# mLSTM with top-1 MoE: list scatters once per group, and transposed columns through a PSUM bank of their own

## The chip, the core and the metric

The kernel runs on one core of a Trainium2 chip. The core has a matmul engine (TensorE, PE in the profile; PEld is its weight load), three engines for element-wise work (VectorE or DVE, ScalarE or ACT, GpSimd or POOL) and SyncE (SP), which here only starts transfers. Each engine runs its own instructions in order and waits on semaphores of the others. Matmuls write to PSUM, a small memory of banks, from which DVE and ACT read. POOL also issues the indirect transfers (gathers and scatters by a list of addresses).

The metric is the device time of one execution in microseconds (us). Lower is better.

## The reference

Two steps. First a recurrent attention (mLSTM) over 4 batches of 8 heads, 768 steps, 40 values per head. Then its output, as 3072 tokens of 320 values, goes through a mixture of experts that gives each token one of 8 experts, with a hidden width of 1024:

```python
logits = x @ w_gate + modality_bias[modality_id]
e_idx = np.argmax(logits, axis=1)
...
gate_w = probs[np.arange(N), e_idx]
for e in range(E):
    mask = e_idx == e
    h = np.maximum(x[mask] @ w1[e], 0.0)
    out[mask] = gate_w[mask, None] * (h @ w2[e])
```

`modality_id` is 0 or 1 for each token, and the bias of its modality mostly decides the expert.

## The kernel before

**Tiles.** Attention runs in 24 units of 128 rows and writes rows of x to DRAM (`x_d`), sorted by modality. As the bias mostly decides, the kernel does not wait for the logits: for each of the two modalities it deals six tiles of 256 tokens to that modality's usual expert, loads that expert's weights early, and multiplies while the logits are still being verified. The 12 dealt tiles are numbered 0 to 11 here. A token that turns out to want another expert (a "bad" one), and every token beyond the sixth tile of its modality, is entered in a list in DRAM (`list_d`), and two leftover tiles of 128 tokens ("slots") gather their tokens from it at the end, with weights that are loaded once the list says which experts they need.

**An expert tile** is 64 matmuls `h_ps` (L1012) in four chunks of 16, each followed by ACT's relu `hh` (L1015) and DVE's low part `hl` (L1016), then 48 matmuls `o_ps` (L1030) in four pieces of 12, and for each of its two halves of 128 tokens ACT's scaling `ob` (L841) and a scatter to `out` on POOL (L842). Between these eight pieces the code advances all other work once; such a step is a half-beat here, so a tile lasts eight of them.

**The work beside it** is a set of generators which `together()` advances once per half-beat each, in the order of the list `threads`. The order of the instructions on each engine is this order of writing: nothing moves them later. The ones that matter here:

- `load_work` loads a tile's tokens from `x_d` into `xg` (SP).
- `column_work(0)` and `column_work(1)`, for the even and odd tiles, run `column_steps`: ACT scales each half to a high part (`xr`/`ex`, L868), DVE makes the low part (two operations per half, L873), PE transposes five blocks into PSUM (`xTg_ps`, L480), and DVE copies them out as `xT` (L886). The transposes take a buffer of the pool `psY`, tag "y", of two buffers, which is also that of `o_ps`; `opend` and `y_last` keep a transpose from taking the second buffer while an `o_ps` is being summed.
- `verify_work` computes the logits of a group of tiles and marks `bad`; `list_work` runs `lists`, which ranks the bad tokens of the group by expert (matmuls L968 and L970, DVE L974 to L980) and scatters into `list_d`, one indirect transfer on POOL per half (L985). Addresses of tokens that aren't bad lie out of bounds and are dropped. The groups hold columns j = 0, 1, 2, 3, then 4 and 5 together, then 6 (the tokens beyond): 4 halves each, 8 in the fifth.
- `rest_work` waits for the last rank, computes the slots' expert numbers and counts (`work_list`, some 30 small DVE operations and the matmul of `nvds`, L721), then gathers the slots' tokens (L830) and makes their columns. `weight_work` starts the slots' weights as soon as the expert numbers are there: SP's transfers into `ws`, ACT's high part (L789), DVE's low part (L790).

If the list overflows what two slots can hold, a register `todo_i` sends the program into further code at its end. With the inputs used here it doesn't: four tokens in all are entered in the list, at most one of them in any partition of a group.

Of the kernel before, what the change touches and what calls it, by code (L numbers as in the profile page):

```python
# [20 lines left out]
P = 128  # L21
# [43 lines left out]
def kernel(  # L65
# [514 lines left out]
    def constants():  # L580
# [19 lines left out]
        g.memset(bases[:, NMOD:], float(NTOK))  # L600
        one_e = one_t[:, 0:E]
# [35 lines left out]
    def work_list(l, run, used, nk, nm):  # L637
# [80 lines left out]
        l.update(nv=nvi)  # L718
        yield "pe"
        nv_b = nvb[:, 0:nk]  # L720
        nc.tensor.matmul(nv_b, lhsT=ones[0:nk], rhs=nvd[0:nk, 0:nk], start=True, stop=True, skip_group_check=True)  # L721
# [5 lines left out]
        if nm == "s":  # L727


            nv_r, m = nv_b[0:1], cst.tile([1, 4], F32, name="more")  # L730
            v.tensor_copy(m[:, 0:1], nv_r[:, 2 * TS:2 * TS + 1])
            v.tensor_scalar(m[:, 1:2], nv_r[:, 0:1], -float(P), 0.0, ALU.add, ALU.max)
            v.tensor_tensor(m[:, 2:4], bases[0:1, 1:], ends[0:1], ALU.subtract)
            more = cst.tile([1, 1], F32, name="more1")
            v.tensor_reduce(more, m, axis=AX.X, op=ALU.max)
            v.tensor_scalar(todo_i, more, 1.0, None, ALU.min)
# [66 lines left out]
    def group(t, ks, js, nm):  # L803
# [4 lines left out]
                 ent=xp.tile([P, a, r, 2], I32, name="entr" + nm, bufs=1), mb=mb_sb[:, ks[0]:ks[0] + a], a=a, r=r, nm=f"{a}{r}", tls=[])  # L808
# [37 lines left out]
    def column_steps(tl, tight=False):  # L846


        nonlocal y_last
# [15 lines left out]
        if not tight:  # L865
            yield
        for h in range(nh):
            nc.scalar.mul(xrs[h][:, 0:DM], xg[:, h, 0:DM], sc[:, h:h + 1].bitcast(F32))  # L868
        if not tight:
            yield  # L870
        for h in range(nh):
            for a, z, o in ((2 * P, DM, DM), (0, 2 * P, 3 * P)):
                nc.vector.scalar_tensor_tensor(xrs[h][:, o:o + z - a], xg[:, h, a:z], sc[:, h:h + 1].bitcast(F32), xrs[h][:, a:z],  # L873
                                               ALU.mult, ALU.subtract)
        tl["split"] = True
        yield
        for h in range(nh):

            while opend and not y_last:
                yield  # L880
            ps = psY.tile([P, 5, P], F16, name="xTg_ps", tag="y")
            y_last = False
            transposes(xrs[h], ps)
            if not tight:
                yield
            nc.vector.tensor_copy(xT[:, :, h], ps)  # L886
        yield
# [63 lines left out]
    def lists(g, each=1):  # L951
# [27 lines left out]
        slot_i = sm.tile([P, n], I32, name="sloti" + nm)  # L979
        v.tensor_tensor(slot_i, slot, flat(off), ALU.add)  # L980
        g["ranked"] = True
        yield
        ent = g["ent"].rearrange("p a r w -> p (a r) w")
        for h in range(n):
            disjoint("list", nc.gpsimd.indirect_dma_start(  # L985
                out=list_d[:, :], out_offset=bass.IndirectOffsetOnAxis(ap=slot_i[:, h:h + 1].bitcast(U32), axis=0),
                in_=ent[:, h], in_offset=None, bounds_check=E * LCAP - 1, oob_is_err=False))
            if h % each == each - 1:
                yield

    h_pools = (psS, "s"), (psG, "g")

    opend = y_last = False
# [25 lines left out]
    def layer2(wts, tl, hid, halves):  # L1019

        nonlocal opend, y_last
        w2h, w2l = wts[2:4]
        hh, hl = hid
        for q, h in enumerate(halves):
            hs = slice(q * P, (q + 1) * P)
            o_ps = psY.tile([P, DM], F32, name="o_ps", tag="y")
            opend = y_last = True
# [9 lines left out]
            opend = False  # L1037
# [34 lines left out]
    run = cst.tile([P, E], F32, name="run")  # L1072

# [291 lines left out]
    def leftover():  # L1365

        v = nc.vector
        n = NTOK // T
# [53 lines left out]
    def still_state():  # L1422
# [183 lines left out]
        def load_work():  # L1606
            for x, (i, j, k) in enumerate(order):
# [5 lines left out]
                if i not in gs:  # L1613
                    gs[i] = group(tab, range(NMOD), sets[i], str(i))
# [7 lines left out]
        def column_work(q):  # L1622
            for x, (i, j, k) in enumerate(order):
# [8 lines left out]
                for _ in column_steps(tl, not over):  # L1632
# [15 lines left out]
        def list_work():  # L1648
            for i, js in enumerate(sets):
                while i not in gs or "verified" not in gs[i]:  # L1650
                    yield
                for _ in lists(gs[i], 2 if att_over else 1):
# [212 lines left out]
```

## Time and profile before

| | us |
|---|---|
| three runs | 326.4, 323.12, 323.44 |
| their median | 323.44 |
| the profiled execution | 320.36 |
| its span, first to last instruction | 318.6 |
| PE, DVE, ACT, POOL busy | 268.0, 169.9, 125.4, 121.0 |
| tile 6 starts | 176.10 |
| tile 10 starts | 260.10 |
| the slots' matmuls start | 290.8 |

A row of a timeline gives the start in us, the duration in us, the engine, the line, the operation with what it writes and reads, how many were merged, and in brackets the idle time ahead of it with what ended it. "<-issue" means that nothing in the profile explains the idle time, "<-remote" that the releaser couldn't be named. The granted clock of PE is 1 at full speed.

### The profile page before, as it was taken

Reading aid. Unit: us, or ns where it says so; the run is one execution under the profiler, and the core shown is the slowest. Engines: PE = TensorE matmul, PEld = TensorE weight load, DVE = VectorE, ACT = ScalarE, POOL = GpSimd, SP = SyncE. Lnnn points to the kernel's source line nnn. Section 1 sums busy time; section 2 is a strip of 40 time slices with the busy share of each in tenths; the row PEclk is TensorE's granted clock in tenths of the full one; section 3 lists DMA queues with packets and bytes.
Section 4 is the critical chain, followed back from the end, with each engine's and each line's share of the span. In section 5 each row is a group of like instructions: output and inputs, shape, how many; then the busy total and the mean of one; then the engine's idle time right before and its main releaser. Section 6 shows DMA issues by size and latency. Waiting matters only on the chain.

```text
span 318.6 us, 6393 instructions
## 1 busy us (share of the span) xinstructions
PE 268.0 (84%) x2384; PEld 210.8 (66%) x2384; DVE 169.9 (53%) x551; ACT 125.4 (39%) x230; POOL 121.0 (38%) x177
## 2 busy tenths in 40 slices
PE   8797986897999999897989959399997889979920
PEld 3475764885887889686866736387976468858810
DVE  7756786489473577329344546137531637775200
ACT  7427565375543455344132413022320226862200
POOL 8734452334755266442582103401137342303110
PEclk9999799799999999999999979789999599999995
DMA  6699968623561461051141411100001068851000
GB/s 176 169 287 335 279 199 272 229 70 114 167 186 62 127 187 41 23 158 53 41 127 41 128 40 36 50 0 23 23 2 41 0 176 197 278 204 43 2 11 0
DMA packets 17354, 36.63 MB, mean 115 GB/s; under 512 B 4439, under 2 KB 8505, under 8 KB 17314
## 3 DMA queue, kind: packets, MB, share of 16 engines
q1 hardware_dynamic: 13922, 27.90, 29.4%
q0 software_dynamic: 3392, 8.24, 7.6%
q8 instruction: 20, 0.33, 0.5%
q14 instruction: 20, 0.16, 0.2%
HBM read 27.90 MB, written 8.57 MB: 114 GB/s over the span
## 4 chain that ended last, share of the span: by engine, by line
PE 40%; DVE 17%; DMA 16%; issue 9%; ACT 6%; another core or an unknown queue 4%; POOL 3%; SPq 1%; POOLq 0%; ACTq 0%; DVEq 0%
PE o_ps L1030 15%; PE h_ps L1012 15%; DMA ws<-in_w 4%; DVE hl L1016 3%; DMA wx<-bp_d 3%; PE xTg_ps L480 3%; DMA kt<-in_kv 2%; PE y_ps L1488 2%; DMA sg<-in_og 2%; ACT hh L1015 2%; DVE ex L873 2%; DMA wx<-in_steps_c 2%; DVE wx L790 2%; PE ubank L892 1%
## 5 line engine op out<-in xcount | busy, mean ns | idle before, releaser
L1012 PEld LDWEIGHTS <-wx 128*128 128x128 f16 x896 | 82.8, 100 | 17.4 <-issue 7.4
L1030 PE MATMUL o_ps<-wx,hh 128*128 128x320 f16 x416 | 87.5, 304 | 3.3 <-DVE eb L886 1.9
L1016 DVE SCALAR_TENSOR_TENSOR hl<-h_ps,hh 128x512 f16<-128x512 f32 x52 | 35.8, 689 | 83.1 <-ACT hh L1015 58.1
L1012 PE MATMUL h_ps<-xT,wx 128*128 128x256 f16 x512 | 62.3, 280 | 2.9 <-DVE hl L1016 2.1
L1030 PE MATMUL o_ps<-wx,hl 128*128 128x320 f16 x208 | 63.0, 303 | 0.0
L1015 ACT ACTIVATE hh<-h_ps 128x512 f16<-128x512 f32 x52 | 30.9, 594 | 69.2 <-PE h_ps L1012 55.1
L842 POOL DMA_INDIRECT out<-ob,oi x24 | 25.7, 1069 | 83.5 <-ACT ob L841 75.7
L1030 PEld LDWEIGHTS <-hh 128*128 128x128 f16 x416 | 40.0, 100 | 19.4 <-issue 3.7
L1477 POOL TENSOR_TENSOR so<-sg,den 128x320 f32<-128x320 f32 x24 | 22.0, 915 | 58.2 <-DVE den L1473 45.9
L985 POOL DMA_INDIRECT list_d<-entr,sloti x28 | 27.9, 995 | 21.4 <-DVE key L927 9.8
L841 ACT ACTIVATE ob<-o_ps,entr 128x320 f32<-128x320 f32 x24 | 12.6, 526 | 56.3 <-PE o_ps L1030 53.9
L790 DVE SCALAR_TENSOR_TENSOR wx<-ws,wx 128x768 f16<-128x768 f32 (+1 forms) x24 | 26.8, 1125 | 8.7 <-ACT wx L789 5.8
L1140 PE MATMUL warm_ps<-warm 128*128 128x512 bf16 x101 | 27.4, 412 | 1.4 <-POOL neg L1197 1.4
L470 POOL DMA_INDIRECT x_d<-row,place_i x24 | 24.6, 1027 | 5.9 <-issue 4.3
L1030 PEld LDWEIGHTS <-hl 128*128 128x128 f16 x208 | 20.6, 99 | 8.4
L789 ACT ACTIVATE wx<-ws 128x768 f16<-128x768 f32 (+1 forms) x24 | 23.4, 978 | 6.0 <-DMA ws<-in_w 5.8
L1012 PE MATMUL h_ps<-eb,wx 128*128 128x256 f16 x192 | 23.4, 277 | 2.6 <-issue 2.6
L480 PE MATMUL xTg_ps<-ident_h,ex 128*128 128x128 f16 x110 | 11.0, 236 | 16.3 <-DVE eb L886 7.2
L480 PEld LDWEIGHTS <-ex 128*128 128x128 f16 x110 | 8.4, 106 | 19.2 <-issue 8.5
L1488 PE MATMUL y_ps<-wx,eb 80*128 80x82 f32 x160 | 20.8, 273 | 0.0
L1488 PEld LDWEIGHTS y_ps<-wx,eb 80*128 80x128 f32 x160 | 20.2, 194 | 0.8
L438 ACT ACTIVATE sg<-sg 128x960 f32<-128x960 f32 x16 | 15.9, 993 | 6.0 <-DMA sg<-in_og 5.9
(242 smaller groups left out, 305.5 us busy)
## 6 DMA issues: line engine op xcount, KB each, us to landing
ws<-in_w SPq DMA_DIRECT2D x16, 384.0 KB
ws<-in_w SPq DMA_DIRECT2D x8, 640.0 KB
xg<-x_d SPq DMA_DIRECT2D x14, 322.0 KB
sg<-in_og SPq DMA_DIRECT2D x8, 480.0 KB
eb<-in_ql SPq DMA_DIRECT2D x8, 320.0 KB
kt<-in_kv SPq DMA_DIRECT2D x4, 324.0 KB
wx<-in_qk SPq DMA_DIRECT2D x8, 160.0 KB
wx<-in_steps_c SPq DMA_DIRECT2D x2, 320.0 KB
```

The source lines that it names most:

```text
L470: ins = nc.gpsimd.indirect_dma_start(out=x_d[:, :], out_offset=bass.IndirectOffsetOnAxis(ap=place_i[:, n:n + 1].bitcast(U32), axis=0), in_ ...
L480: nc.tensor.transpose(dst[:, i], row[:, i * P:(i + 1) * P], ident_h)
L789: nc.scalar.mul(wh, w, WSC)
L790: lows.append(lambda wl=wl, w=w, wh=wh: nc.vector.scalar_tensor_tensor(wl, w, WSC, wh, ALU.mult, ALU.subtract))
L842: disjoint("out", nc.gpsimd.indirect_dma_start(out=out[:, :], out_offset=bass.IndirectOffsetOnAxis(ap=oi.bitcast(U32), axis=0), in_=ob, in ...
L985: disjoint("list", nc.gpsimd.indirect_dma_start(out=list_d[:, :], out_offset=bass.IndirectOffsetOnAxis(ap=slot_i[:, h:h + 1].bitcast(U32), ...
L1012: nc.tensor.matmul(h_ps[:, i], lhsT=l, rhs=r, start=(i == 0 and q == 0), stop=(i == g - 1 and q == 7), skip_group_check=True)
L1015: nc.scalar.activation(hh[:, sl, 0:n], h_ps, AF.Relu)
L1016: nc.vector.scalar_tensor_tensor(hl[:, sl, 0:n], h_ps, 0.0, hh[:, sl, 0:n], ALU.max, ALU.subtract)
L1030: nc.tensor.matmul(o_ps, lhsT=l[:, fc, hs], rhs=r[:, fc], start=(fc == 0 and i == 0), stop=(fc == NFC - 1 and i == 2))
L1140: nc.tensor.matmul(ps, lhsT=warm[:, 0:P], rhs=warm, start=True, stop=True, skip_group_check=True)
L1488: nc.tensor.matmul(y_ps[:, 2 * p:2 * p + 2], lhsT=qat[n][0:2 * D, p], rhs=bds[n // NCH][0:2 * D, p], start=(p == 0), stop=(p == NP - 1), s ...
```

## The change

**One scatter per group.** `lists` still ranks every half, but writes the addresses of all halves to a table that is kept (`slot_all`, beside the entries in `ent_all`). For each partition DVE then takes the smallest address of the group (addresses of tokens that aren't bad are huge), masks the entry that belongs to it, sums it out over the group, and POOL scatters that one entry per partition: 6 scatters in place of 28. If any partition of any group holds two bad tokens, `worst` is above 1; a matmul of `over` = (worst > 1) with ones brings that to all partitions, `more` takes it in, every entry of the slots is padded out (`pad`) and the code at the end scatters all 28 and does the rest. With these inputs this isn't reached.

**Columns.** `column_steps` is rewritten: once the dealt tiles run (`over`), a tile's column work begins on half-beats of parity 0 or 1 by tile, so that two tiles alternate; it goes half by half (ACT's high part of the next half beside DVE's low part of this one), and a half's five transposes and their copy (`turn`) stand together in one half-beat. They use the pool `psM`, tag "misc", which has one buffer and which the attention's exponents use until `heavies_over`. The guard of `opend` and `y_last` is gone. After the attention, ACT copies the even halves out and DVE the odd ones. The columns made ahead of the first tile, and those of the slots, still go through `psY`, and the slots' copies stay on DVE.

The core of the diff:

```diff
@@ constants @@
+        g.memset(worst, 0.0)
+        g.memset(slot_all, float(BIG))
+        g.memset(ent_all, 0)
@@ work_list @@
+        if nm == "s":
+            ov = cst.tile([P, 1], BF16, name="over")
+            v.tensor_scalar(ov, worst, 1.0, None, ALU.is_gt)
         yield "pe"
         nv_b = nvb[:, 0:nk]
+        if nm == "s":
+            nc.tensor.matmul(lgps[1][:, NTILE:NTILE + 1], lhsT=ones, rhs=ov, start=True, stop=True, skip_group_check=True)
         nc.tensor.matmul(nv_b, lhsT=ones[0:nk], rhs=nvd[0:nk, 0:nk], start=True, stop=True, skip_group_check=True)
...
+            v.tensor_copy(m[:, 4:5], lgps[1][:, NTILE:NTILE + 1])
...
+            v.tensor_scalar(pad, pad, more, None, ALU.max)
@@ column_steps, from its second step on @@
+        def turn(h, pool, tag, copy):
+            ps = pool.tile([P, 5, P], F16, name="xTg_ps", tag=tag)
+            transposes(xrs[h], ps)
+            copy(xT[:, :, h], ps)
...
+        yield
+        high(0)
         yield
         for h in range(nh):
-
-            while opend and not y_last:
-                yield
-            ps = psY.tile([P, 5, P], F16, name="xTg_ps", tag="y")
-            y_last = False
-            transposes(xrs[h], ps)
-            if not tight:
-                yield
-            nc.vector.tensor_copy(xT[:, :, h], ps)
-        yield
+            low(h)
+            if h + 1 < nh:
+                high(h + 1)
+            else:
+                tl["split"] = True
+            yield
+
+            turn(h, psM, "misc", nc.scalar.copy if both_engines and h % 2 == 0 else nc.vector.tensor_copy)
+            yield
@@ lists @@
-        slot_i = sm.tile([P, n], I32, name="sloti" + nm)
-        v.tensor_tensor(slot_i, slot, flat(off), ALU.add)
+        v.tensor_tensor(slots, slot, flat(off), ALU.add)
+        one, c = sm.tile([P, 2], F32, name="one1"), sm.tile([P, 1], F32, name="cbad")
+        s1 = one[:, 1:2]
+        v.tensor_reduce(s1, slots, axis=AX.X, op=ALU.min)
+        v.tensor_reduce(c, g["bad"], axis=AX.XY, op=ALU.add)
+        v.tensor_tensor(worst, worst, c, ALU.max)
         g["ranked"] = True
         yield
+        sel = sm.tile([P, n], I32, name="sel" + nm)
+        v.tensor_scalar(sel, slots, s1, -1.0, ALU.is_equal, ALU.mult)
+        both_ = sm.tile([P, n, 2], I32, name="selb" + nm)
+        v.tensor_tensor(both_, ent, sel.rearrange("p n -> p n ()").broadcast_to([P, n, 2]), ALU.bitwise_and)
+        e1 = sm.tile([P, 3], I32, name="ent1")
+        v.tensor_reduce(one[:, 0:1], both_[:, :, 0], axis=AX.X, op=ALU.add)
+        v.tensor_reduce(e1[:, 1:2].bitcast(F32), both_[:, :, 1].bitcast(F32), axis=AX.X, op=ALU.add)
+        v.tensor_copy(e1[:, 0:3:2], one)
+        yield
+        scatter_all(e1[:, 0:2].rearrange("p w -> p () w"), e1[:, 2:3], 1)
@@ column_work @@
-                for _ in column_steps(tl, not over):
+                while over and (now % 2 != q or not heavies_over):
+                    yield
+                for _ in column_steps(tl, not over, att_over):
@@ list_work @@
-                for _ in lists(gs[i], 2 if att_over else 1):
+                for _ in lists(gs[i]):
```

What this moves, at three places. POOL's order from the third-last group of scatters on, before (`out` rows are the scatters of the expert tiles, `xg` the gather of the slots' tokens):

```order
L842 DMA out<-ob,oi_1978 3072x320
L985 DMA list_d<-entr_1979,sloti_2832 28672x2 x2
L842 DMA out<-ob,oi_1978 3072x320
L985 DMA list_d<-entr_1979,sloti_2832 28672x2 x2
L842 DMA out<-ob,oi_1978 3072x320 x2
L985 DMA list_d<-entr_2351,sloti_3334 28672x2 x2
L842 DMA out<-ob,oi_2350 3072x320
L985 DMA list_d<-entr_2351,sloti_3334 28672x2 x4
L842 DMA out<-ob,oi_2350 3072x320
L985 DMA list_d<-entr_2351,sloti_3334 28672x2 x2
L985 DMA list_d<-entr_2723,sloti_3501 28672x2 x4
L842 DMA out<-ob,oi_2350 3072x320 x2
```

and in the changed kernel, the same stretch:

```order
L856 DMA out<-ob,oi_1981 3072x320 x2
L1037 DMA list_d<-ent_2857 28672x2
L856 DMA out<-ob,oi_1981 3072x320 x2
L856 DMA out<-ob,oi_2367 3072x320 x2
L1037 DMA list_d<-ent_3438 28672x2
L856 DMA out<-ob,oi_2367 3072x320
L1037 DMA list_d<-ent_3571 28672x2
L856 DMA out<-ob,oi_2367 3072x320 x2
L844 DMA xg_99<-x_d,li 128x322
```

Sixteen scatters of three groups become three, with scatters to `out` between them. DVE's order around tiles 6 and 7, before (`hl` belongs to the expert tile, `xr`, `ex` and the copies from `xTg_ps` to the columns of later tiles):

```order
L1016 SCALAR_TENSOR_TENSOR hl_96<-h_ps,hh_94 128x512
L873 SCALAR_TENSOR_TENSOR xr_128<-xg_97,sc,xr_128 128x64
L873 SCALAR_TENSOR_TENSOR xr_128<-xg_97,sc,xr_128 128x256
L873 SCALAR_TENSOR_TENSOR ex_110<-xg_97,sc,ex_110 128x64
L873 SCALAR_TENSOR_TENSOR ex_110<-xg_97,sc,ex_110 128x256
L873 SCALAR_TENSOR_TENSOR ex_111<-xg_98,sc,ex_111 128x64
L873 SCALAR_TENSOR_TENSOR ex_111<-xg_98,sc,ex_111 128x256
L873 SCALAR_TENSOR_TENSOR ex_112<-xg_98,sc,ex_112 128x64
L873 SCALAR_TENSOR_TENSOR ex_112<-xg_98,sc,ex_112 128x256
L886 COPY sg_122<-xTg_ps 128x5x128
L886 COPY sg_123<-xTg_ps 128x5x128
```

and in the changed kernel:

```order
L1064 SCALAR_TENSOR_TENSOR hl_96<-h_ps,hh_94 128x512
L883 SCALAR_TENSOR_TENSOR ex_110<-xg_98,sc,ex_110 128x64
L883 SCALAR_TENSOR_TENSOR ex_110<-xg_98,sc,ex_110 128x256
L1064 SCALAR_TENSOR_TENSOR hl_96<-h_ps,hh_94 128x512
L889 COPY eb_120<-xTg_ps 128x5x128
L883 SCALAR_TENSOR_TENSOR ex_111<-xg_99,sc,ex_111 128x64
L883 SCALAR_TENSOR_TENSOR ex_111<-xg_99,sc,ex_111 128x256
L1064 SCALAR_TENSOR_TENSOR hl_96<-h_ps,hh_94 128x512
```

The low parts of two tiles stood in one block of eight and their copies in pairs; now each half's low part and copy lie between two `hl`, and half of the copies are gone from DVE. The third place is DVE ahead of tile 10, before (the numbers of the slots, then tile 10's `hl` and the first weights):

```order
L733 TENSOR_TENSOR more<-bases,taken 1x2
L735 TENSOR_REDUCE more_3639<-more 1x1
L736 TENSOR_SCALAR todo_i<-more_3639 1x1
L739 TENSOR_SCALAR padis<-pads 128x52
L1016 SCALAR_TENSOR_TENSOR hl_95<-h_ps,hh_93 128x512 x2
L790 SCALAR_TENSOR_TENSOR wx_108<-ws_105,wx_108 128x3x256
```

and in the changed kernel:

```order
L1064 SCALAR_TENSOR_TENSOR hl_95<-h_ps,hh_93 128x512
L733 TENSOR_TENSOR pads<-pos_f,ubank 128x52
L739 COPY more<-ubank 128x1
L740 TENSOR_SCALAR more<-ubank 128x1
L741 TENSOR_TENSOR more<-bases,taken 128x2
L742 COPY more<-ubank 128x1
L744 TENSOR_REDUCE more_3685<-more 128x1
L745 TENSOR_SCALAR more_3685<-more_3685 128x1
L746 CAST todo_i<-more_3685 1x1
L748 TENSOR_SCALAR pads<-pads,more_3685 128x52
L751 TENSOR_SCALAR padis<-pads 128x52
L1064 SCALAR_TENSOR_TENSOR hl_95<-h_ps,hh_93 128x512 x3
```

The slots' numbers now end behind the first `hl` of tile 10 instead of ahead of it, and the first weights stand behind all four. In all, DVE has 46 rows more than before, the tiles start at the same half-beats as before, the last group's rank stands two half-beats later than before, and so do the work list, the gathers of the slots' tokens and their weights.

71 lines of the change are left out of this document (44 added, 27 removed).

## The prediction

> **What bounds the kernel now.** I read the page first, then the table of windows cut at the starts of tiles, then the timelines of POOL, ACT and PE inside the windows that lose time, and last the chain behind the two leftover slots.
>
> ```profile
> span 318.6 us, 6393 instructions
> ...
> PE 268.0 (84%) x2384; PEld 210.8 (66%) x2384; DVE 169.9 (53%) x551; ACT 125.4 (39%) x230; POOL 121.0 (38%) x177
> ...
> PE 40%; DVE 17%; DMA 16%; issue 9%; ACT 6%; another core or an unknown queue 4%; POOL 3%; SPq 1%; POOLq 0%; ACTq 0%; DVEq 0%
> ...
> L985 POOL DMA_INDIRECT list_d<-entr,sloti x28 | 27.9, 995 | 21.4 <-DVE key L927 9.8
> ```
>
> PE is busy 84% of the span, so a change that removes no matmul can only win PE's idle time and the time in which its clock is lowered. The 28 list scatters cost POOL 27.9 us of its 121.0; POOL has room, so their busy time alone is worth nothing. "Another core or an unknown queue" holds 4% of the chain, 12.7 us: this kernel has one core, so it stands for waits whose releaser the view could not name. The windows (us, then PE, PEld, DVE, ACT and POOL busy, granted clock, DMA share) show where PE loses time late in the kernel; they are tiles 6 to 10, the stretch up to the slots, and the slots:
>
> ```profile
> 176.10:199.10 23.00, 17.97 (x153) 13.33 (x150) 13.07 (x53) 7.49 (x16) 3.60 (x4) 0.93 0.23 67
> 199.10:223.60 24.50, 19.03 (x210) 15.38 (x208) 10.71 (x35) 4.72 (x9) 4.32 (x5) 0.86 0.07 24
> 223.60:238.20 14.60, 14.60 (x158) 12.04 (x156) 6.66 (x29) 3.82 (x8) 3.41 (x4) 1.00 0.04 12
> 238.20:260.10 21.90, 17.78 (x122) 12.16 (x120) 8.51 (x50) 3.44 (x6) 12.31 (x13) 0.84 0.16 44
> 260.10:273.30 13.20, 13.20 (x112) 10.71 (x110) 7.65 (x9) 7.53 (x11) 4.25 (x4) 1.00 0.84 244
> 273.30:290.80 17.50, 14.70 (x125) 11.55 (x123) 12.95 (x23) 10.97 (x15) 3.75 (x2) 1.00 0.53 179
> 290.80:304.70 13.90, 13.87 (x180) 11.78 (x177) 3.26 (x5) 3.44 (x6) 1.97 (x2) 1.00 0.05 16
> ```
>
> Tile 10 runs without a stall: 13.20 us, clock 1.00. Tiles 6, 7 and 9 take 23.00, 24.50 and 21.90. PE's idle time in tiles 6 to 9 is 84.00 - (17.97 + 19.03 + 14.60 + 17.78) = 14.6 us, and tiles 6, 7 and 9 are also those with a clock under 1.00. What PE waits for there, with its slow work beside it:
>
> ```profile
> 185.34 0.93 PE L480 MATMUL xTg_ps<-ident_h,ex 128*128 128x128 f16 x10 [2.05 <-DVE eb L886]
> 186.10 3.43 PE L1012 MATMUL h_ps<-xT,wx 128*128 128x256 f16 x16
> 191.43 0.43 PE L1030 MATMUL o_ps<-wx,hh 128*128 128x320 f16 x2 [1.90 <-DVE eb L886]
> ...
> 199.13 1.91 PE L1012 MATMUL h_ps<-xT,wx 128*128 128x256 f16 x16
> 206.18 1.25 PE L480 MATMUL xTg_ps<-ident_h,ex 128*128 128x128 f16 x10 [5.13 <-DVE eb L886]
> 207.22 5.00 PE L1012 MATMUL h_ps<-xT,wx 128*128 128x256 f16 x31
> ...
> 245.14 0.61 PE L1012 MATMUL h_ps<-eb,wx 128*128 128x256 f16 x4 [0.40 <-issue]
> ...
> 248.69 1.74 PE L1012 MATMUL h_ps<-eb,wx 128*128 128x256 f16 x7 [1.13 <-issue]
> 250.22 0.74 PE L1030 MATMUL o_ps<-wx,hh 128*128 128x320 f16 x2
> ...
> 254.22 0.60 PE L1030 MATMUL o_ps<-wx,hh 128*128 128x320 f16 x2
> ...
> 256.57 0.17 PE L721 MATMUL ubank<-nvds,ones 26*128 26x26 bf16 x1 [0.80 <-DVE nvds L715]
> ```
>
> The three largest waits end with the copy of a transposed column (L886) out of the PSUM buffer that it shares with o_ps: 2.05, 1.90 and 5.13 us. The 5.13 has a second cause, which the timelines of ACT and POOL show:
>
> ```profile
> 204.40 0.60 ACT L1015 ACTIVATE hh<-h_ps 128x512 f16<-128x512 f32 x1 [5.59 <-remote]
> ...
> 248.71 0.60 ACT L1015 ACTIVATE hh<-h_ps 128x512 f16<-128x512 f32 x1 [7.22 <-remote]
> ```
>
> ```profile
> 197.16 1.05 POOL L985 DMA_INDIRECT list_d<-entr,sloti x1 [0.30 <-issue]
> ...
> 202.37 0.98 POOL L985 DMA_INDIRECT list_d<-entr,sloti x1 [0.30 <-issue]
> ...
> 235.17 0.98 POOL L985 DMA_INDIRECT list_d<-entr,sloti x1 [9.76 <-DVE key L927]
> ...
> 246.76 0.98 POOL L985 DMA_INDIRECT list_d<-entr,sloti x1 [0.31 <-issue]
> 252.01 0.98 POOL L985 DMA_INDIRECT list_d<-entr,sloti x1 [4.27 <-DVE cnts L644]
> ...
> 255.87 0.98 POOL L985 DMA_INDIRECT list_d<-entr,sloti x1 [0.30 <-issue]
> ```
>
> At 199.13 a chunk of 16 matmuls starts and takes 1.91 us, so its data is there at 201.04; ACT takes it at 204.40, 3.36 us late, 1.05 us after the burst that ended at 202.37 + 0.98. The second time hh starts at 248.71, 0.97 us after the burst that ended at 246.76 + 0.98. So both unexplained waits end about 1 us after a run of back-to-back indirect DMAs. This is co-occurrence, not proof, and the burst of 252.01 to 256.85 shows no such wait.
>
> **The change, part by part.** The sum is made on the profiled execution, 320.36 us (its span of 318.6 and 1.8 around it); the three runs have a median of 323.44, 3.1 above it. I take the difference from the sum off the median.
>
> *Lowered clock.* A chunk of 16 takes 1.91 us at full clock and 3.43 at 186.10: 1.5 lost. The 31 at 207.22 take 5.00 where 31/16 of 1.91 is 3.7, and the transposes 1.25 for 0.93: 1.6 lost. From 250.22 to 254.22 layer 2 runs at half clock, 2.0 lost, and the 7 at 248.69 take 1.74 for 7/16 of 1.91, 0.9 lost. Together 6.0. The granted clock of that stretch:
>
> ```profile
> 250.22:254.22 4.00, 4.00 (x16) 2.21 (x15) 3.79 (x23) 0.60 (x1) 1.91 (x2) 0.50 0.01 0
> ```
>
> All three stretches follow the idle time above, so they go if it goes. At stake in tiles 6 to 9: 14.6 + 6.0 = 20.6 us.
>
> *Scatters, 28 to 6.* Four to one per group, twelve to two for the last two groups: no burst stays, since two scatters never follow one another (POOL's order above). If the bursts cause the late hh, this gives 3.36 us in tile 7 and, in tile 9, the 15 matmuls from 245.14 to the end of the row at 248.69: 5.3 us where 15/16 of 1.91 is 1.8, of which 0.9 was counted as clock, so 2.6. I take this cause (both ends agree to 0.1 us), and price the other in the first rival.
>
> *Columns in their own bank, one turn per half-beat.* The waits of 2.05 and 1.90 end with a copy out of the shared buffers, and o_ps itself stands behind one of them; with its own bank a transpose no longer holds o_ps up. But the bank is one: a turn waits for the copy of the turn before. What that costs is not in the trace. From below: nothing, when half-beats of 13.20/8 = 1.65 us leave the copy its time. From above: 1.9 to 2.05, the waits of now. What stands ahead of the copy on DVE prices it (groups by shape: busy us, mean ns of one, idle before):
>
> ```profile
> L1016 DVE SCALAR_TENSOR_TENSOR hl<-h_ps,hh 128x512 f16<-128x512 f32 x52 | 35.8, 689 | 83.1 <-ACT hh L1015 58.1 <-issue 25.0
> ...
> L873 DVE SCALAR_TENSOR_TENSOR ex<-xg,sc,ex 128x256 f16<-128x256 f32 x22 | 10.5, 478 | 0.0
> ...
> L886 DVE COPY xT<-xTg_ps 128x640 f16<-128x640 f16 x16 | 7.5, 478 | 2.0 <-PE xTg_ps L480 0.9 <-remote 0.9
> ...
> L873 DVE SCALAR_TENSOR_TENSOR ex<-xg,sc,ex 128x64 f16<-128x64 f32 x22 | 6.5, 297 | 1.3 <-ACT ex L868 1.3
> ...
> L975 DVE TENSOR_TENSOR run<-ubank,run 128x8 f32<-128x8 f32 x6 | 1.0, 166 | 0.2
> ```
>
> One hl (0.69), one low half (0.48 + 0.30) and the copy (0.48) make 1.95 us, 0.3 over a half-beat. I take 0.3 for each of the 8 turns in tiles 6 to 9, 2.4 us, nearer the lower end because the even copies go to ACT, whose busy time there is 19.5 of 84 us.
>
> *New DVE rows, 46.* About eight small operations per group; by the 0.166 us of L975, one of their kind, 7.6 us in all. DVE is busy 39.0 of 84.0 us in tiles 6 to 9, which covers them, except at the last group. There 44 operations (7.3 us) lead from the rank to `over`, and PE has two matmuls for them (`over`, then L721) ahead of tile 10. Before, PE waits 0.80 us there. Now the rank stands two half-beats later in the order, five into tile 9: 5 x 1.65 + 7.3 = 15.6 us after its start, where PE without stalls has 13.2 and about 1 of other small matmuls. I take a wait of 1.4; the ends are 0, if the rank comes as early as now, and 1.4 + 3.3 = 4.7, if it slips by two half-beats more.
>
> *So tiles 6 to 9 keep 2.4 + 1.4 of 20.6: gain 16.8.*
>
> *Attention stretch.* In the waits of PE after 62 us the column copies of that stretch hold it up in four places; the same change applies, PE is the bound there, and I take half, 1.8:
>
> ```profile
> PE xTg_ps L480 <- DVE xT L886: 3.7, 4, 1.5
> ```
>
> *Start.* Three POOL memsets of some 0.1 us stand ahead of work that waits for DMA: 0.
>
> *Slots.* The work list is ready two half-beats (2 x 1.65 = 3.3 us) later against tile 10's start. Everything behind it moves with it: SP's weight DMAs queued behind the list's numbers, POOL's two gathers, ACT's and DVE's splitting. The chain is tight already:
>
> ```profile
> 264.13 0.83 ACT L789 ACTIVATE wx<-ws 128x768 f16<-128x768 f32 x1
> ...
> 281.97 0.84 ACT L789 ACTIVATE wx<-ws 128x768 f16<-128x768 f32 x1 [2.37 <-DMA ws<-in_w]
> ...
> 285.49 1.27 ACT L789 ACTIVATE wx<-ws 128x1280 f16<-128x1280 f32 x1 [0.18 <-SPq L1786]
> ```
>
> The last weights are split at 286.76, 4 us before the slots' matmuls begin at 290.8. That margin covers part; the transposes of the second slot stand behind the last split on DVE. Loss between 0 and 3.3; I take 2.9, because ACT waits for the weights as they come.
>
> *Sum:* 16.8 + 1.8 - 2.9 = 15.7. That is 304.7 on the profiled execution and 307.7 on the median; rounded, 307.5.
>
> **Rivals.** *First: the bursts are not the cause.* For it: the burst of 252.01 passed without a late semaphore, and POOL and ACT share no data there. Then 3.4 + 2.6 and the clock behind them, 1.6 + 2.9, stay: 10.5 less gain, 5.2 in all, 318.2. Against it: two waits, both ending 1.0 us after a burst. The Trainium skill, in "SBUF — State Buffer", section "Who interferes with whom", says "PE and ACT never wait on anyone" and lets only DVE and GpSimd lock each other out; by that rule the bursts could not hold ACT, and this rival holds. The late hh of 204.40 and 248.71 neither confirm nor break it, since what is late may be a semaphore rather than an operand.
>
> *Second, the other side: the one bank is slower than the shared two.* Some 20 turns (ten tiles by two) wait for the copy before. Without waits the gain is 15.7 + 2.4 = 18.1, so it turns into a loss from 0.9 us a turn on. At 1.2 us, about the DVE queue of one hl and one copy (0.69 + 0.48), 20 turns cost 24.0 and the time is 323.4 + 5.9 = 329.3. For it: 1.90 and 2.05 were waited behind such copies with two buffers. Against it: those turns came two in a row, now a half-beat lies between. The Trainium skill, "TensorE: Matmul & The Clock Gate", section "A second HAM failure mode: psum-queue depth-cycling", has PE's short idles between groups bring its clock down; the 3.43 us chunk behind a 2.05 us wait agrees, and by it this rival's turning point would come earlier than 0.9.
>
> *Third: the slots set the end.* If the weights move by all of 3.3 us and the second slot's transposes by as much again, the loss is 6.6 instead of 2.9: 311.4.
>
> **Chances.** Forecast 0.60, first rival 0.20, second 0.07, third 0.13. The forecast's own range: no wait at turns and no loss at the slots, gain 21.0, 302.4; turns at 0.8 (6.4) and nothing in the attention stretch, gain 9.9, 313.5. The range reaches over the first rival (318.2) by 1.3, for waits at turns beside it, and downward to what the attention stretch (the other 1.9) and PE's idle time of 273.30 to 290.80 (2.8) could add to the 302.4: 297.7, rounded 297.5. A measurement of this kernel tells about 1% (3.2 us) from no change, so faster means under 320.2: 0.83, with a part of the first rival (waits that stay a little longer) within 1%: 0.09, slower 0.08.
>
> **What would show it.** Right: no hh wait "<-remote" over 1 us after 176 us; tiles 6 to 9 together near 67 us (84.0 now) at clock 1.00; waits of L480 for a copy under 0.5 us each; tile 10 beginning near 241.5 us; the slots' matmuls 33.6 us later rather than 30.7. Wrong: late hh beside single scatters (first rival); many waits of L480 near 1 us with the clock at 0.5 behind them (second); slots that begin over 36 us after tile 10 (third).

## The result and the profile after

The changed kernel takes 299.8 us (median of 4 runs, 298.4 to 301.35) beside 324.92 us before (4 runs, 323.12 to 327.79): a ratio of 0.922, 95% interval 0.913 to 0.931. The profiled execution takes 299.97 us with a span of 298.2, so 20.4 us less than the profiled one before. Medians here are of all runs, while a ratio leaves out runs over 1.5% above the fastest of their kernel, so it need not be the quotient of two medians. One sentence on the change above isn't right: the slots' columns go through the new bank too; only the columns made ahead of the first tile stay in `psY`.

The page after, its first lines, and the group of the list scatters:

```profile
span 298.2 us, 6406 instructions
...
PE 266.6 (89%) x2385; PEld 211.5 (71%) x2385; DVE 174.2 (58%) x597; ACT 129.7 (44%) x236; POOL 97.0 (33%) x158
```

```profile
L1037 POOL DMA_INDIRECT list_d<-ent x6 | 6.0, 994 | 4.9 <-DVE ent L1030 3.8 <-issue 0.8 <-DVE cis L682 0.3
```

PE's work is the same (266.6 for 268.0 us); what went is its idle time and the low clock. POOL lost 22 scatters of about a microsecond. The windows of the changed kernel, cut at the starts of tiles (attention beside tiles 0 to 5, then tiles 6 to 10, the stretch up to the slots, the slots):

```profile
68.84:176.90 108.06, 104.41 (x997) 87.55 (x996) 67.43 (x248) 50.08 (x101) 46.18 (x63) 1.00 0.34 105
176.90:192.72 15.82, 15.30 (x144) 12.23 (x141) 11.17 (x50) 6.78 (x14) 1.97 (x2) 1.00 0.30 86
192.72:208.80 16.08, 15.99 (x171) 13.14 (x169) 7.62 (x25) 7.86 (x15) 2.95 (x3) 1.00 0.14 42
208.80:225.25 16.45, 16.36 (x206) 13.63 (x204) 8.93 (x36) 4.98 (x10) 1.97 (x2) 1.00 0.06 21
225.25:240.35 15.10, 14.16 (x122) 11.16 (x119) 11.46 (x68) 4.09 (x8) 4.20 (x5) 1.00 0.07 23
240.35:253.87 13.52, 13.52 (x114) 10.97 (x114) 7.41 (x18) 5.84 (x9) 2.62 (x3) 1.00 0.64 202
253.87:272.79 18.92, 14.94 (x125) 11.52 (x123) 14.02 (x24) 12.60 (x17) 4.15 (x5) 1.00 0.66 215
272.79:286.62 13.83, 13.82 (x178) 11.74 (x176) 3.26 (x5) 2.92 (x5) 1.07 (x2) 1.00 0.05 15
```

Tiles 6, 7 and 9 took 23.00, 24.50 and 21.90 us at clocks of 0.93, 0.86 and 0.84; now they take 15.82, 16.08 and 15.10 at 1.00. PE's idle time in tiles 6 to 9 is 63.45 - 61.81 = 1.6 us where it was 14.6. Most of what is left is in two rows of PE's timeline, a turn that waits for the copy ahead of it and the wait for `over`:

```profile
187.38 0.44 PE L480 MATMUL xTg_ps<-ident_h,ex 128*128 128x128 f16 x5 [0.38 <-DVE eb L889]
...
240.14 0.16 PE L728 MATMUL ubank<-over,ones 128*128 128x1 bf16 x1 [0.94 <-DVE over L724]
```

In the list of waits (sum, times, longest), ACT's hh waits for an unnamed releaser four times in the kernel before:

```profile
ACT hh L1015 <- PE h_ps L1012: 55.1, 38, 5.6
...
ACT hh L1015 <- remote: 13.9, 4, 7.2
```

In the changed kernel no such row is left; the only one for hh is:

```profile
ACT hh L1063 <- PE h_ps L1060: 52.6, 45, 4.4
```

### The profile page after: what moved, and what is told of

Read it like the earlier page. It is cut to its first block, busy times and chain, and to the rows that moved or that the text cites. A ratio compares the mean times of both kernels' runs of the same rounds, so it can differ in the third digit from the quotient of the medians.

```text
span 298.2 us, 6406 instructions
## 1 busy us (share of the span) xinstructions
PE 266.6 (89%) x2385; PEld 211.5 (71%) x2385; DVE 174.2 (58%) x597; ACT 129.7 (44%) x236; POOL 97.0 (33%) x158
## 5 line engine op out<-in xcount | busy, mean ns | idle before, releaser
L1076 PE MATMUL o_ps<-wx,hh 128*128 128x320 f16 x416 | 85.6, 299 | 0.0
L1060 PE MATMUL h_ps<-xT,wx 128*128 128x256 f16 x512 | 59.8, 274 | 0.8 <-DVE hl L1064 0.7
L856 POOL DMA_INDIRECT out<-ob,oi x24 | 24.0, 999 | 93.0 <-ACT ob L855 86.6
L855 ACT ACTIVATE ob<-o_ps,entall 128x320 f32<-128x320 f32 x24 | 12.6, 527 | 52.4 <-PE o_ps L1076 43.9
L1189 PE MATMUL warm_ps<-warm 128*128 128x512 bf16 x101 | 29.8, 439 | 1.5 <-POOL neg L1246 1.4
L1540 PEld LDWEIGHTS y_ps<-wx,eb 80*128 80x128 f32 x160 | 21.7, 207 | 1.1 <-issue 0.3
L1540 PE MATMUL y_ps<-wx,eb 80*128 80x82 f32 x160 | 22.3, 286 | 0.0
L1060 PE MATMUL h_ps<-eb,wx 128*128 128x256 f16 x192 | 21.8, 273 | 0.0
L1189 PEld LDWEIGHTS <-warm 128*128 128x128 bf16 x101 | 11.0, 115 | 12.6 <-issue 4.8
L467 ACT ACTIVATE ya<-row 128x320 f16<-128x320 f32 x24 | 11.2, 467 | 19.0 <-DVE row L1534 13.4
```

The costliest lines, as they stand in the source:

```text
L856: disjoint("out", nc.gpsimd.indirect_dma_start(out=out[:, :], out_offset=bass.IndirectOffsetOnAxis(ap=oi.bitcast(U32), axis=0), in_=ob, in ...
L1060: nc.tensor.matmul(h_ps[:, i], lhsT=l, rhs=r, start=(i == 0 and q == 0), stop=(i == g - 1 and q == 7), skip_group_check=True)
L1076: nc.tensor.matmul(o_ps, lhsT=l[:, fc, hs], rhs=r[:, fc], start=(fc == 0 and i == 0), stop=(fc == NFC - 1 and i == 2))
L1189: nc.tensor.matmul(ps, lhsT=warm[:, 0:P], rhs=warm, start=True, stop=True, skip_group_check=True)
L1540: nc.tensor.matmul(y_ps[:, 2 * p:2 * p + 2], lhsT=qat[n][0:2 * D, p], rhs=bds[n // NCH][0:2 * D, p], start=(p == 0), stop=(p == NP - 1), s ...
```

## The experiments

Three batches ran on three chips, one batch on each, numbered 10, 8 and 4 in the runs; the chip of the result is not recorded. The kernel before doesn't take the same time on all of them, which turned out to be the main finding:

| chip | kernel before, median us (runs) | others there, median us |
|---|---|---|
| of the result | 324.92 (4) | changed 299.8 |
| 10 | 312.63 (13) | lists only 317.33, columns only 305.83, copies on DVE 299.54, any half-beat 307.45 |
| 8 | 324.25 (10) | before again 323.66, changed 299.97, bursts 316.51, tail 297.78 |
| 4 | 312.88 (13) | spaced 302.56, fewer memsets 296.39, lists only 315.39, columns only 306.55 |

**The two halves of the change, apart.** Lists only, as a diff against the changed kernel:

```diff
-            turn(h, psM, "misc", nc.scalar.copy if both_engines and h % 2 == 0 else nc.vector.tensor_copy)
+            while opend and not y_last:
+                yield
+            ps = psY.tile([P, 5, P], F16, name="xTg_ps", tag="y")
...
-                while over and (now % 2 != q or not heavies_over):
-                    yield
```

> The kernel before with one list scatter per group, its columns as before (shared buffers, pairs of tiles). Theory (the bursts of indirect scatters make ACT's hh late): no hh waits more than 1 us for a releaser that can't be named after 176 us; the freezes and the clock behind them (3.4 + 2.6 + 1.6 + 2.9 = 10.5 us) go, the waits of 2.05 and 1.90 for column copies stay; 324.9 - 10.5 = about 314 us. Rival (the late hh has to do with the shared PSUM buffers): the long waits stay, about 325 us, or up to 328 with the extra DVE rows.

Measured: 317.33 us beside 312.63 us of the kernel before on that chip, ratio 1.026 (1.009 to 1.043): slower, though perhaps by less than 2%. There are no late hh, but the kernel before doesn't seem to pay for any there either, so removing bursts won nothing, and the longer DVE chain ahead of `over` (the small operations of rank and work list) shows on PE:

```profile
246.85 0.16 PE L728 MATMUL ubank<-over,ones 128*128 128x1 bf16 x1 [4.26 <-DVE over L724]
```

With the old columns the chain ends 4.26 us after PE asks for it, and PE then runs at a granted clock of 0.50 for 5.85 us; with the new ones it is 0.94. The traces show why: the order differs. Here the last rank stands ahead of tile 9, DVE's part of it waits 3.02 us behind that tile's first hl, and the `over` matmul stands behind the four chunks, which take PE 7.15 us. In the changed kernel the rank stands behind the four chunks and `over` ahead of tile 10, so that the whole second layer, 48 `o_ps`, covers the chain. The waits for column copies are where they were (2.05, 1.90 and 1.81 us in tiles 6 and 7). Neither theory had this outcome.

Columns only is the rest of the diff:

```diff
-            scatter_all(e1[:, 0:2].rearrange("p w -> p () w"), e1[:, 2:3], 1)
+        for h in range(n):
+            disjoint("list", nc.gpsimd.indirect_dma_start(
...
+            if h % each == each - 1:
+                yield
```

> The kernel before with the new columns (bank of their own, opposite half-beats, even copies on ACT), its lists as before (28 scatters, two per half-beat late). Theory (bursts): hh is late again by 2 us or more behind at least one burst; the time lies about 10 us above the changed kernel, near 310 us. Rival (shared buffers): no late hh, within 3 us of the changed kernel, 297 to 303 us.

Measured: 305.83 us, ratio 0.986 (0.975 to 0.996). The time lies between both expectations; the trace decides. POOL has its bursts, the longest of eight in a row, and ACT's hh starts on time in the middle of it:

```profile
223.90 0.98 POOL L998 DMA_INDIRECT list_d<-entr,sloti x1 [0.30 <-issue]
...
232.91 0.98 POOL L998 DMA_INDIRECT list_d<-entr,sloti x1 [0.30 <-issue]
...
255.29 1.10 POOL L830 DMA_INDIRECT xg<-x_d,li x1 [0.30 <-issue]
```

```profile
225.25 0.60 ACT L1028 ACTIVATE hh<-h_ps 128x512 f16<-128x512 f32 x1 [1.03 <-PE h_ps L1025]
227.00 0.60 ACT L1028 ACTIVATE hh<-h_ps 128x512 f16<-128x512 f32 x1 [1.15 <-PE h_ps L1025]
228.75 0.60 ACT L1028 ACTIVATE hh<-h_ps 128x512 f16<-128x512 f32 x1 [1.15 <-PE h_ps L1025]
```

The hh are 1.75 us apart, a chunk each. So a burst alone doesn't make hh late. What columns only loses to the changed kernel, it loses from tile 10 on. There the work list comes late, and PE waits for it inside the tile, which takes 17.76 us for 13.52:

```profile
241.16 0.17 PE L721 MATMUL ubank<-nvds,ones 26*128 26x26 bf16 x1 [2.31 <-DVE nvis L717]
```

The gathers begin at 255.29, 20.1 us after tile 10's start at 235.19 (12.6 us in the changed kernel: 252.95 and 240.35), and the slots' matmuls 39.7 us after it (32.4). The 12 scatters of the last two groups stand ahead of the gathers, but it is not their time that counts: POOL then idles 8.36 us. The gathers are written later, and so stand behind both of tile 10's scatters to `out`; in the changed kernel only one is ahead of them.

On chip 4, where the kernel before takes 312.88 us, both ran once more:

> The kernel before with one list scatter per group and its old columns, once more, for a chip where the kernel before takes about 324 us. If there the late hh are what the scatters cost: 314 to 319 us, as on the chip before, and so 5 to 10 us less than the kernel before, though it was 5 more there. If not: 324 or more.

> The kernel before with the new columns and its 28 scatters, once more, for a chip where the kernel before takes about 324 us. If bursts make hh late there whatever the columns: late hh of 2 to 4 us behind bursts, 312 to 320 us. If the shared buffers were needed for it: about 306 us, as on the chip before.

315.39 us (ratio 1.010, 1.003 to 1.017) and 306.55 us (0.973, 0.967 to 0.980), so the same again, and no word on a chip where hh is late.

**What makes the columns fast.** All copies on DVE:

```diff
-            turn(h, psM, "misc", nc.scalar.copy if both_engines and h % 2 == 0 else nc.vector.tensor_copy)
+            turn(h, psM, "misc", nc.vector.tensor_copy)
```

> The changed kernel with all column copies on DVE. If the copy behind hl and the low half on DVE sets the wait at the bank (0.3 us for each turn, as the prediction priced it), about 8 to 10 turns that were ACT's gain such a wait: 302 to 304 us. If the half-beat leaves room enough: 299 to 301 us.

299.54 us: the copies may stand on either engine. The changed kernel was not run on this chip; beside its profile on chip 8, tile 6 takes 16.61 us for 15.82 and tiles 7 to 10 are equal to 0.02 us. Turns in any half-beat:

```diff
-                while over and (now % 2 != q or not heavies_over):
+                while over and not heavies_over:
```

> The changed kernel with the columns of both tiles free to start in any half-beat, so that two turns can stand in one half-beat and the second waits at the one bank for the first one's copy. If the opposite half-beats are what makes one bank enough: waits of PE for column copies of 0.5 to 1.5 us at each such pair, 303 to 310 us with the clock behind them. If the bank alone brought the gain: 299 to 301 us.

307.45 us, 7.9 more than the run with all copies on DVE beside it. The waits at the one bank are there, and the matmuls after the second one run slowly:

```profile
180.38 0.44 PE L480 MATMUL xTg_ps<-ident_h,ex 128*128 128x128 f16 x5 [0.78 <-ACT eb L889]
...
186.87 0.44 PE L480 MATMUL xTg_ps<-ident_h,ex 128*128 128x128 f16 x5 [2.01 <-DVE eb L889]
...
188.58 0.74 PE L1076 MATMUL o_ps<-wx,hh 128*128 128x320 f16 x2
...
201.18 0.44 PE L480 MATMUL xTg_ps<-ident_h,ex 128*128 128x128 f16 x5 [1.30 <-DVE eb L889]
```

Pairs of `o_ps` take 0.74 us, as in the half-clock stretch of the kernel before, where 0.43 is usual. Tiles 6 and 7 together take 7.4 us more than with all copies on DVE (20.27 and 19.86 for 16.61 and 16.09); this is the price of the turns, and the opposite half-beats are what makes a single bank enough there. Tile 9 takes 4.2 us more (19.26 for 15.10), and that is another wait, since this edit moves the list chain in the order as well:

```profile
244.74 0.16 PE L728 MATMUL ubank<-over,ones 128*128 128x1 bf16 x1 [3.42 <-DVE over L724]
```

The stretch from tile 10 to the slots wins 2.3 back. So the 7.9 us are not the bank's alone. The Trainium skill, "TensorE: Matmul & The Clock Gate", section "A second HAM failure mode: psum-queue depth-cycling", says that short idles between groups can bring the clock down; this run agrees, with a granted clock of 0.71 from 187.14 to 193 us behind the wait of 2.01 us.

**Bursts and chips.** The kernel before again, and the changed kernel, on one chip:

> The kernel before, unchanged, looked at again, since its time beside the first four experiments was 312.6 us where it had been 323 to 328. If the late hh are the difference: on a chip where it takes about 312 us, no hh waits over 1 us for an unnamed releaser after 176 us and tile 7 and tile 9 are some 5 and 6 us shorter (19 to 20 and 16 to 17 us); on a chip where it takes about 324, both long waits are there again. If the difference lies elsewhere (the start, the slots): tiles 6 to 9 take 84 us in both.

> The changed kernel, unchanged, so that it, the kernel before and the next two are compared on one chip. If the late hh belong to a chip and not to the kernel: where the kernel before takes about 312 us, this one takes about 300, a ratio of 0.96; where it takes about 324, again about 300, a ratio of 0.92.

This was chip 8: 324.25 us and 299.97 us, ratio 0.937 (0.921 to 0.953). The late hh are there again (ACT's timeline of the kernel before on chip 8, then the last scatter of each burst from POOL's):

```profile
206.44 0.60 ACT L1015 ACTIVATE hh<-h_ps 128x512 f16<-128x512 f32 x1 [4.21 <-remote]
...
249.89 0.60 ACT L1015 ACTIVATE hh<-h_ps 128x512 f16<-128x512 f32 x1 [6.50 <-remote]
```

```profile
205.81 0.98 POOL L985 DMA_INDIRECT list_d<-entr,sloti x1 [0.30 <-issue]
...
248.67 0.98 POOL L985 DMA_INDIRECT list_d<-entr,sloti x1 [0.30 <-issue]
```

The first starts 0.35 us before the end of its burst, the second 0.24 us behind it. So the 1.05 and 0.97 us of the prediction's profile, which agreed so well, don't come again; that hh waits beside a burst does.

The windows of both (attention with tiles 0 to 5, tiles 6 to 9, tile 10 up to the slots, the slots), first the kernel before on chip 8, then the changed one:

```profile
65.55:181.05 115.50, 104.84 (x998) 87.46 (x997) 64.69 (x224) 49.88 (x101) 55.41 (x72) 1.00 0.32 97
181.05:264.46 83.41, 67.78 (x630) 51.64 (x627) 38.92 (x166) 19.36 (x39) 23.70 (x24) 0.94 0.16 48
264.46:294.22 29.76, 28.10 (x237) 22.45 (x235) 20.58 (x31) 18.53 (x27) 7.64 (x6) 1.00 0.60 189
```

```profile
67.42:174.86 107.44, 103.92 (x998) 87.29 (x997) 67.39 (x248) 50.08 (x101) 46.19 (x63) 1.00 0.34 105
174.86:238.31 63.45, 61.82 (x632) 50.21 (x628) 39.16 (x178) 23.72 (x46) 11.05 (x12) 1.00 0.14 43
238.31:270.96 32.65, 28.45 (x235) 22.47 (x235) 21.45 (x41) 18.43 (x26) 6.78 (x7) 1.00 0.67 208
```

In the same batch, bursts put back into the changed kernel, with addresses out of bounds so that nothing else changes:

```diff
         scatter_all(e1[:, 0:2].rearrange("p w -> p () w"), e1[:, 2:3], 1)
+        if g["bad"] is not g["val"]:
+            for _ in range(n - 1):
+                scatter_all(e1[:, 0:2].rearrange("p w -> p () w"), far, 1)
```

> The changed kernel with the scatters of the first five groups followed by 3 (fifth group: 7) more to addresses out of bounds, back to back, so that POOL has bursts of 4 and 8 again. Theory that bursts by themselves make hh late: long unnamed waits of hh of 2 to 4 us behind bursts, 303 to 310 us, on any chip. Theory that it takes a chip on which semaphores come late: no such wait and within 1.5 us of the changed kernel where the kernel before takes about 312 us; late hh only where it takes about 324.

Measured: 316.51 us, 16.5 more than the changed kernel on that chip, from 19 scatters on an engine that has room. POOL, then ACT, in the first of the places:

```profile
163.03 0.98 POOL L1041 DMA_INDIRECT list_d<-ent x1 [0.30 <-issue]
...
166.89 0.98 POOL L1041 DMA_INDIRECT list_d<-ent,far x1 [0.30 <-issue]
...
168.87 1.02 POOL L470 DMA_INDIRECT x_d<-row,place_i x1 [0.16 <-issue]
```

```profile
163.97 0.60 ACT L1067 ACTIVATE hh<-h_ps 128x512 f16<-128x512 f32 x1 [0.70 <-PE h_ps L1064]
...
170.40 0.60 ACT L1067 ACTIVATE hh<-h_ps 128x512 f16<-128x512 f32 x1 [5.39 <-remote]
...
248.84 1.11 ACT L856 ACTIVATE ob<-o_ps,entall 128x320 f32<-128x320 f32 x2 [8.19 <-remote]
```

The hh at 170.40 belongs to tile 5's third chunk, whose matmuls end at 165.68, so it is 4.72 us late; tile 5 takes 21.49 us for 15.14 in the changed kernel, tile 7 18.56 for 16.09, tile 9 18.11 for 15.09. Behind the burst of eight it is not hh that comes late but the two `ob` (the first sum ends at 243.28), so it isn't a matter of one line: what PE signals arrives late. PE itself also stands still there, 0.45, 0.99 and 0.87 us between matmuls of one sum, with nothing named. Of the 16.5 us, 2.4 lie behind the last matmul, as they do on a chip without late signals (the next run).

The semaphore records of the traces, which the views don't print, bear this out. In the kernel before, PE's record for the chunk that ends at 201.04 stands at 204.38, just ahead of the late hh; in this run those for 165.68 and 167.43 stand at 170.38 and 170.54. They also tell the chips apart. On chip 8 and that of the result, 33 to 79 of some 900 signals of DVE, ACT and PE in each of six profiles have no record within 0.25 us of the end of their instruction, each of them within 2.6 us of the start of an indirect transfer, single ones included. In the eight profiles on chips 10 and 4 it is 2 of 7176. For DVE and ACT it seems to be the record alone that is missing (here DVE's hl at 164.60 follows in time on ACT's hh of 163.97, whose signal has none); for PE it is often the signal that is late. So recording, too, suffers there, and whether it has a part in the delay no run here tells. The same 19 extra scatters, one at a time in every second half-beat:

```diff
-            for _ in range(n - 1):
-                scatter_all(e1[:, 0:2].rearrange("p w -> p () w"), far, 1)
+            pend.extend([e1] * (n - 1))
...
+                if pend and now % 2:
+                    scatter_all(pend.pop(0)[:, 0:2].rearrange("p w -> p () w"), far, 1)
```

> The run with bursts again (19 scatters to addresses out of bounds beside the 6), but the extra ones one at a time, in every second half-beat. If it is the back-to-back run that makes semaphores late: within 3 us of the changed kernel, 300 to 303 us, and no hh late by over 1 us. If each scatter costs its share wherever it stands: near the 316.5 us of the bursts. On a chip where the kernel before takes about 312 us no verdict: 300 to 303 either way.

302.56 us, on chip 4, where the kernel before takes 312.88: no verdict, as the expectation says. It does show that the scatters' own price is small: no tile is longer by more than 1.6 us than on chip 8 without them, and from the last matmul to the end it is 14.06 us for 11.52, which is nearly all of the difference of 2.6.

**The tail and the start.** The matmuls of `over` and nvds a half-beat later, and the slots' columns earlier:

```diff
-                if p == "wait" or i % 6 == 5:
+                if p in ("pe", "wait") or i % 6 == 5:
...
-            for _ in range(2):
-                yield
             for _, tl in slots:
```

> The changed kernel with the matmuls of over and nvds one half-beat later, and the slots' columns two half-beats earlier. If the wait for over (0.94 us) and the waits of the slots' transposes (1.91, 1.01 and 0.73 us) lie on the path: 1 to 3 us less than the changed kernel. If weights set the slots' start: no more than 1 us less.

297.78 us (296.19 to 298.91) beside 299.97 (298.04 to 302.79): 2.2 less, between runs that overlap by under 1 us. The wait for `over` is gone and tile 9 takes 13.78 us for 15.09; the stretch up to the slots gains 0.3 (32.31 for 32.65), which speaks for weights, not columns, setting the slots' start. The slots' matmuls themselves take 15.45 us for 13.83 in its profile, at a granted clock of 0.80 in the first slot, behind a wait of 1.79 us; that takes back most of it.

```diff
-        g.memset(slot_all, float(BIG))
-        g.memset(ent_all, 0)
```

> The run with the later matmuls and earlier slots' columns, without the memsets of the two tables at the start (every entry is written before it is read). If the memsets delay the first tile: 1 to 3 us less than that run's 297.8 us, and tile 0 before 66 us. If the first tile's start varies with the transfers: 297 to 299 us.

296.39 us, but on another chip, so the 1.4 us are not told from it; tile 0 begins at 68.15 us in it, no earlier than with the memsets (66.0 to 68.8). Both are versions that are as fast as the changed kernel or a little faster.

## Why the prediction was right

It gave 307.5 us and a gain of 15.7; measured are 299.8 and 25.1 between the medians. The 299.8 lie inside the wide range, but below the forecast's own (302.4 to 313.5). Of the 25.1, 20.4 are between the profiled executions; the rest is that the profiled execution of the kernel before, 320.36, lies 4.6 under its median. By stretches of the profiled executions (gain in us, a loss is negative):

| step of the prediction | forecast | chip of the result | chip 8 |
|---|---|---|---|
| start, up to tile 0 | 0 | -6.3 | -1.9 |
| attention stretch, tiles 0 to 5 | 1.8 | 5.5 | 8.1 |
| tiles 6 to 9 | 16.8 | 20.6 | 20.0 |
| tile 10 up to the slots' matmuls | -2.9 | -1.7 | -2.9 |
| after the last matmul | none named | 2.3 | 2.4 |
| sum of the span | 15.7 | 20.4 | 25.6 |

- *Bursts make hh late.* On two chips the mechanism was right: it goes with the bursts and comes back with them (16.5 us for 19 scatters, 14.1 of them before the last matmul). That both ends agreed to 0.1 us, on which the prediction took this cause, was luck: on chip 8 they lie 0.35 us before and 0.24 us behind the end of the burst. "No burst stays" was too strong as well: scatters to `out`, gathers and list scatters still follow each other, four in a row from 251.66 us on in the result's profile. Yet hh is never over 0.84 us late in the changed kernel, on chip 8 or that of the result. As a statement about the kernel alone it was wrong: with 28 scatters in bursts hh was never more than 0.04 us late on chips 10 and 4, so the first rival's doubt was justified, though not its outcome. Its own evidence, the burst of 252.01, told nothing: no hh is due between 250.46 and 261.89 in that profile. The prediction priced all of it at 10.5 us; the kernel before is 324.25 - 312.88 = 11.4 us slower on chip 8 than on chip 4, the size of that price. That this difference is the late hh was not shown by a trace of the kernel before on chips 10 or 4, which wasn't taken; lists only and columns only weren't run on a chip with late hh either, so how the gain there divides between the halves isn't measured. What differs between the chips stays open, and since each had one batch, whether it is the chip or the hour; so does whether 19 spaced scatters are harmless where hh is late. The Trainium skill, "SBUF — State Buffer", section "Who interferes with whom", has PE and ACT never wait for another engine's port; ACT's 3.36 us were not a wait at a port but for a signal that had not come, which that rule leaves untouched.
- *Columns: the term of 2.4 us.* It was mis-sized. Eight turns at 0.3 were forecast; tiles 6 to 9 have twelve, in the kernel before too, and 0.38 in all was measured. The price added hl, low half and copy into one half-beat; with opposite half-beats the turn of one tile and the low half of the other meet another hl, and the copy is done before the bank is asked for again. The reason given for the low end, even copies on ACT, was wrong: with all copies on DVE the time is 299.54 us. The second rival's mechanism is real: it makes tiles 6 and 7 longer by 7.4 us as soon as the half-beats are no longer opposite.
- *Attention stretch: the term of 1.8 us.* Mis-sized by 4 to 6. Half of four copy waits was taken. Where hh isn't late, the new columns take 106.7 us from tile 0 to tile 6 and the old ones 109.5 and 110.4, so the columns give some 3. The rest may be late signals there too, which the prediction had priced in tiles 7 and 9 alone: the kernel before has hh late by 0.5 to 1.4 us six times in this stretch, between 86 and 168 us. How much of the 8.1 on chip 8 they are was not measured.
- *The wait for over:* 1.4 forecast, 0.94 measured. Its upper end of 4.7 is nearly what lists only pays (4.26), but by chance: the prediction let the rank slip later, and there it stands earlier in the order. What covers the chain is its place behind the first layer of tile 9, which the half-beats of the new columns give it.
- *The slots:* 2.9 forecast, 1.7 and 2.9 measured.
- *The start:* 0 forecast; tile 0 began 6.3 us later in the result's profile, 1.9 on chip 8. Over all profiles with the 28 scatters' code at the start it lies at 62.5 to 66.8, with the memsets at 66.0 to 68.8, and without two of three at 68.2. SP issues the load of the first tokens (`xg`) at 51.63 us in the result's profile and at 47.34 in the one before, so 4.3 of the 6.3 are there by then; a cause in the change isn't shown.
- *The end:* not seen. It is in the last section.

That both halves are needed was in none of the steps. On the chips without late hh, lists only loses 2.5 to 4.7 us, columns only wins 6.3 to 6.8, and both together 13.1 (by the run with copies on DVE, 299.54 for 312.63). Each half alone puts the list's chain at a place in the order where PE waits for it: `over` inside tile 9 in the one (4.26 us), `nvds` inside tile 10 and the late gathers in the other (2.31 us).

## What to carry to other kernels

A wait whose releaser can't be named and that ends behind a run of indirect transfers is worth the experiment of adding transfers to nowhere, and of running the kernel before on more than one chip: the same program differed by 12 us here. An edit that moves one generator by a half-beat moves others in the order too, so every wait in the trace has to be read before a difference is put down to the edit. One PSUM buffer is enough for two producers when their turns lie in opposite half-beats and each is copied out before the next. Two edits that each look small or harmful alone can cover each other's new wait, so they have to be timed together as well as apart.

## What the runs showed of the hardware

- *Signals from PE can be late behind back-to-back indirect transfers of POOL, on some chips.* From the moment when a chunk's matmuls are done and ACT is free, to its hh, it is up to 6.86 us in the kernel before (241.85 to 248.71), 4.72 in the run with bursts and 0.84 in the changed kernel; never more than 0.04 us on chips 10 and 4 in any of the eight profiles there. The number of transfers in a row doesn't set it alone: the 0.84 us come behind a row of four on chip 8, the 6.86 inside a longer one.
- *Each indirect transfer costs 0.1 us at the end of the program, also one that moves nothing.* After the last scatter POOL runs two closing steps, whose records (start, duration) in the kernel before and the changed one on chip 8 are

```
before   POOL INC_SWDGE_SEM 312.68 1.78   POOL DRAIN 314.49 6.61
changed  POOL INC_SWDGE_SEM 289.29 1.34   POOL DRAIN 290.66 4.81
```

  together 8.39 and 6.15 us: 2.24 us for 22 transfers fewer. The run with columns only, with 28 scatters on a chip without late hh, has 1.78 and 6.61 as well, and from the last matmul to the end all profiles with 25 or 28 list scatters take 13.8 to 14.1 us, those with 6 take 11.4 to 11.7. In the runs with 25, 19 go to addresses out of bounds.
- *PE's clock fell to half behind waits of about 2 us, but not behind each.* By the traces' clock records it stays at half for 3.4 or 6.8 us at a time. It fell behind 2.05 us in the kernel before, 2.01 in the run with turns in any half-beat and 1.79 in the run of the tail; it did not behind 2.04 us in the kernel before on chip 8 (190.28) and 1.91 in the changed kernel (264.67). So the length of the wait doesn't decide it alone.
